# Moving the ends of attention groups ahead of the next scores, re-weighting the filler matmuls, and letting GpSimd make some shifted copies

## The chip, the cores and the metric

The kernel runs on one core of one Trainium2 chip. The metric is the device time in microseconds, the median of three runs. One more execution was taken with the hardware profiler; it has a time of its own.

## The reference

Four layers work on one sequence of 2048 tokens with 512 features and 32 heads of 16 features, in bf16. Each adds its result to x after a layer norm. Layers 0 and 2 (A) are a segmented attention with a memory; layers 1 and 3 (B) are full attention over all tokens.

```python
x = A_x
x = x + _A_ref(_layernorm(x), A_wq, A_wk, A_wv, A_wo, A_beta)
x = x + _B_ref(_layernorm(x), B_wqkv, B_wo)
x = x + _A_ref(_layernorm(x), A_wq, A_wk, A_wv, A_wo, A_beta)
x = x + _B_ref(_layernorm(x), B_wqkv, B_wo)

def _B_ref(x, wqkv, wo):                    # 32 heads, Dh = 16
    q, k, v = ...
    p = _softmax(einsum('bhqd,bhkd->bhqk', q, k) * Dh ** (-0.5))
    return einsum('bhqk,bhkd->bhqd', p, v) ... @ wo

def _A_ref(x, wq, wk, wv, wo, beta):        # 4 segments of 512 tokens
    for s in range(4):
        p = _softmax(einsum('bhqd,bhkd->bhqk', qs, ks) * scale + causal_mask)
        a_dot = einsum('bhqk,bhkd->bhqd', p, vs)
        a_mem = (phi(qs) @ M) / (phi(qs) @ z + 1e-6)
        outs.append(g * a_mem + (1 - g) * a_dot)
        M, z = M + phi(ks).T @ vs, z + phi(ks).sum(tokens)
    return concat(outs) ... @ wo
```

Almost all of the work is the exponential of the scores: 4096 blocks of 128 keys by 512 queries in the two B layers, and fewer masked ones in the A layers.

## The kernel before, in words

**Groups and units.** A `Group` holds, for a layer, a segment of 512 queries, a block `c` of eight heads and a parity `e`, four heads (`r` = 0 to 3) and all their score blocks, called banks (one bank of PSUM, 128 x 512 in f32). The main loop in `attention` makes one unit per turn. A unit takes up to three banks from the groups in order (`take_banks`); `unit` issues their score matmuls on PE (32 rows of contraction, four heads side by side in the array), then one ACT instruction with the exponential of up to 1536 columns into a slot of `pT`. PSUM has two places for scores, banks 0 to 2 and 4 to 6, used in turn, bank 3 (`DXB`) for projections and extra tiles, and bank 7 (`ACC`), where the products with V (PV) of one group add up. `pT` has four slots (`NPU`).

**PV and group ends.** `pv_step` issues the PV matmuls of banks whose exponential was issued two units earlier (three in A layers). When the last bank of a group is done, `pv_close` calls `finish`, which divides by the row sums on DVE and so frees bank 7; a group that still lacks PV work stays in `self.pend`. Only in groups of layer 3 whose keys are taken in one pass (`fm`) is V the stationary operand with 17 columns (32-column tiles of the array); elsewhere the stationary operand is a 128 x 128 block of `pT`, 51 or 34 columns are streamed, and a bank takes four such matmuls. `finish` ends in line 1378 (or 1354 and 1356, where partial sums are kept); `finish_fm` begins with a transpose in line 1396.

**Exponentials on DVE.** To relieve ACT, some banks get their exponential on DVE. `dx_find` and `dx_take` pick one or two, `dx_first` (line 924) turns scores straight into the bits of a bf16 with a multiply and an add, and `dx_chain` (line 970) makes three further copies with a number of `EXP_D` added; PV is then done with all four, so such a bank costs four times the PV matmuls. `dx_room` lets a unit take such banks only while the planner's DVE time stays within `DQ` of the unit's start. `pv_some` issues the PV matmuls of the copies that are ready by the planner's times; without due banks it stops once PE comes within `PVLATE` of ACT.

**The planner.** `Sched.add` records every operation into its engine's list in the order in which Python calls it, with the semaphore waits that follow from buffers and banks; `estimate` keeps a modelled time per engine, by which the code above chooses. So the order on each engine is fixed when the program is built. Each engine works through its list strictly in order.

**Work between the units.** Projections, layer norms, the A layers' memory, and the output projections are generators run by `background`, some before `pv_step` and some after. `keep_busy` closes each turn: if the planner's weighted sum of streamed columns over the last 3413 ns (`Sched.streamed`) is below `FILL`, it issues up to `FILLS` matmuls with a stationary zero block (128 x 512), into bank 7 of the current group or bank 3.

**GpSimd** makes the causal masks of the A layers (line 1283) and, within the B layers, `qm`, the queries with the other parity's heads set to zero (line 1185). `dx_chain` has a branch to put a copy on it, switched off by `POOL_ON = 0`. That branch is open once the A layer 0 is done (`self.wide`).

In the order of one turn the change touches these lines:

```python
self.compose(n, items)              # scores on PE, exponential on ACT, line 924 on DVE
...
if split and (...):
    self.background(True)
self.cr_dve -= self.pv_step(n)      # PV on PE, finish on DVE
self.run_deferred(False)
self.background(...)
...
self.keep_busy()
```

Of the kernel before, what the change touches and what calls it, by code (L numbers as in the profile page):

```python
# [25 lines left out]
LAG = {"pe": 100, "act": 60, "dve": 60, "pool": 70, "sp": 50}  # L26
# [51 lines left out]
class Sched:  # L78
# [1 line left out]

    CW = 0.5

    def __init__(self):
        self.ops = {e: [] for e in ENGS}
        self.t = {e: 0.0 for e in ENGS}
# [3 lines left out]

    def streamed(self, until, ns):

        while self.streams and self.streams[0][0] < until - ns:
            self.streams.pop(0)
        return sum(w for _, w in self.streams) / ns

    def estimate(self, op, ns, gap, tile):
        e = op.eng
        ready = max([d.end + LAG[d.eng] if d.eng != e else d.end + 35 for d in op.deps], default=0.0)  # L100
        if tile is not None:
            rows, r0, cols, c0, n = tile
            st = max(ready, self.pe_issue())
            if cols < 128:
                st = max(st, self.pe_issue() + 30)
            for (a, ar, b, bc, m, at) in self.tiles:
                if ar < r0 + rows and r0 < ar + a and bc < c0 + cols and c0 < bc + b:
                    st = max(st, at + m / 2.4 + (4 if (a, b) == (rows, cols) else 100))
            self.tiles = self.tiles[-11:] + [(rows, r0, cols, c0, n, st)]
            self.t["pe"] = max(self.t["pe"], st + n / 2.4)  # L110
            self.streams.append((st, n / 2.4 * rows / 128 * max(cols / 128, self.CW)))
            op.end = st + n / 2.4 + 170
        elif e == "sp":
            st = max(ready, self.t[e])
            self.t[e] = st + max(gap, 600)
            op.end = st + ns
        else:
            op.end = self.t[e] = max(self.t[e] + gap, ready + ns)
# [140 lines left out]
class Builder:  # L259
# [3 lines left out]
    PART = 2  # L263
    FILL_DVE = 300
    EARLY = 200
    FILL, FILLS = 0.43, 2
    DVE_FIN, DX_FIN = 600, 2500
    EVAC_ACT = 0
    DX_BANK, DX_LATE, BG_BANK, DVE_LATE, DVE_LATE_LOW = 800, 3000, 200, 1500, 9000000000.0
    CR_A, CR_B, CR_W, CR_LOW, CARRY, CARRY_W, REST, NEAR, SLACK = 1300, 1500, 1400, 2200, 0, 0, 14, 10, 300  # L270
    ALT3, ALT5, GAP, AHEAD, PE_B, PE_A, PE_LOW, LOW, PAIRS, TAKEN, PAIRS2 = 2, 4, 3, 500, 4, 3, 4, 24, 60, 3, 1
    NKS = 6
    DX_T, POOL_T, POOL_ON = 430, 1800, 0
    DQN, TAKEN_N, REST_N, NEAR_N, NEAR_W = 600, 3, 14, 100, 24
    DQ, DXS, PVN, PVLATE, PVWAIT, PVHOLE = 3000, 4, 4, 600, 0, 100
    DMA_STEPS, DMA_LATE = 2, 300

    def __init__(self, nc, A_x, A_wq, A_wk, A_wv, A_wo, A_beta, B_x, B_wqkv, B_wo, out):
# [102 lines left out]
        return DmaBatch(self.dsems[self.ring("dsem", 1 << 30)])  # L381


    def keep_busy(self):


        g, n = self.cur, 0
        own = g is not None and g.npv
        if not own and (self.bank_late() > 0 or any(t["next"][0][:1] == ["cont"] for t in self.tasks)):
            return  # L390
        bank, al = (self.banks[ACC], g.acc) if own else (self.banks[DXB], self.new_alloc())
        while n < self.FILLS and self.sc.streamed(max(self.sc.t["pe"], self.sc.t["act"] - 1330), 3413) < self.FILL:
            self.mm(self.ps[:, bank.col0:bank.col0 + 512], self.zero[:, :], self.wB[:, 0, 0:512], not own, not own,
                    [self.b_zero, self.b_wB[0]], bank, al, "fill")
            n += 1
# [556 lines left out]
    def dx_chain(self, k, b0, ents):  # L952


        n = 512 * len(ents)
        w = self.dx_space(b0)[:, 0:n]
        bw = self.b_dxw[b0][:len(ents)]
        hold = [b0] + [self.dx_bufs.pop(0) for _ in EXP_D[1:]]
        for j in range(1, len(EXP_D)):
            if j > 1:  # L960
                yield [], 0, self.DX_T
            b = hold[j]
            o, d = self.dx_space(b)[:, 0:n], float(EXP_D[j])
            wr = [x for i in range(len(ents)) for x in self.dx_writes(b, i)]
            ns = 435 if len(ents) == 2 else 333
            eng = "dve"
            if self.POOL_ON and self.wide and max(self.sc.t["pool"], bw[-1].last_write.end) + self.POOL_T < self.sc.t["dve"] + self.POOL_ON:
                eng, ns = "pool", self.POOL_T if len(ents) == 2 else 700
            self.dx_todo -= 1
            self.op(eng, (lambda o, d: lambda e: e.tensor_scalar(o, w, d, None, op0=ALU.add))(o, d), reads=bw, writes=wr, ns=ns, name="dxs")  # L970
            self.dx_queue(b, ents, j == len(EXP_D) - 1)
        self.dx_now[k] = []
        self.dx_done(b0)
# [533 lines left out]
    def attention(self):  # L1507
# [22 lines left out]
        n = 0  # L1530
        while True:
# [26 lines left out]
            split = not self.low and not isA  # L1558
            self.unit_no = n
            self.units = n  # L1560
            self.compose(n, items)
            self.credit(self.PE_LOW if self.low else self.PE_A if isA else self.PE_B, self.CR_LOW if self.low else self.CR_A if isA else self.CR_W * len(items) / 3 if self.wide else self.CR_B)
            if split and (not self.FIT or not self.wide or self.FIT & 2):
                self.background(True)
            self.cr_dve -= self.pv_step(n)
            self.run_deferred(False)
            self.background(False if split and not (self.FIT & 1 and self.wide) else None)
            if self.step == 2:
# [57 lines left out]
```

## Time and profile before

| | |
|---|---|
| time, median of three runs | 1962.33 us (1961.81 to 1964.88) |
| the profiled execution's own time | 1963.52 us |
| its span, first to last instruction | 1962.0 us |
| mean granted TensorE clock | 0.969 |
| busy: PE, DVE, ACT, POOL | 1752.8, 1523.5, 1822.8, 286.9 us |
| instructions: PE matmuls, DVE, ACT, POOL | 28190, 3240, 1654, 648 |

PE is the matmul engine, PEld its weight loads, ACT the engine of activations, DVE the vector engine, POOL is GpSimd. A line of a group gives source line, engine, operation, output and inputs, shapes, how many; then busy time in us and the mean of one in ns; then the engine's idle time just before them and who ended it. A line of the waits gives who waited for whom, us in total, how often, the longest. A line of the timeline gives start and length in us, and in brackets the idle time of the engine before it. A line of windows gives the stretch, its length, busy us (with instructions) of PE, PEld, DVE, ACT and POOL, then the granted clock, the DMA share and GB/s. Nearly all matmuls go through one helper, line 398, so that they are told apart by operands and shapes.

### The profile page before, as it was taken

How to read it: one execution, taken by the hardware profiler on the slowest of the kernel's cores; microseconds unless marked ns; L12 is line 12 of the kernel's file. 1: busy time of each engine (PE TensorE's matmuls, PEld its weight loads, DVE VectorE, ACT ScalarE, POOL GpSimd, SP SyncE). 2: the span in 40 equal slices, each digit the busy share in tenths (PEclk: the TensorE clock that was granted, in tenths of full speed). 3: DMA queues.
4: the chain of work that ended last, by engine and by line, in shares of the span. 5: the costliest groups of instructions: out<-in, count | busy, mean ns of one | idle time of the engine just before them, and what ended most of it. 6: DMA issues, size and time to landing. Idle time of an engine off the chain costs nothing.

```text
span 1962.0 us, 64238 instructions
## 1 busy us (share of the span) xinstructions
PE 1752.8 (89%) x28190; PEld 902.2 (46%) x28190; DVE 1523.5 (78%) x3240; ACT 1822.8 (93%) x1654; POOL 286.9 (15%) x648
## 2 busy tenths in 40 slices
PE   7889889899989999799998999899998888888887
PEld 3444444556646665466654666555632222222222
DVE  6656566788748797578875788577999999999996
ACT  6789988889999999999989999888999999999998
POOL 3522153110050000500004100231100000000000
PEclk9889998999999999999999899999999989999999
DMA  5110111000100010100011001010000000000000
GB/s 157 25 31 18 29 21 31 14 10 16 16 13 16 5 17 16 23 13 8 11 21 23 5 6 19 13 21 13 9 18 1 1 1 12 1 1 12 1 2 12
DMA packets 94968, 33.49 MB, mean 17 GB/s; under 512 B 87520, under 2 KB 94176, under 8 KB 94688
## 3 DMA queue, kind: packets, MB, share of 16 engines
q1 hardware_dynamic: 94688, 29.39, 7.6%
q8 instruction: 220, 3.60, 0.8%
q14 instruction: 60, 0.49, 0.1%
HBM read 6.30 MB, written 2.10 MB: 4 GB/s over the span
## 4 chain that ended last, share of the span: by engine, by line
PE 44%; ACT 27%; DVE 17%; issue 9%; DMA 1%; POOL 1%; SPq 0%; ACTq 0%; DVEq 0%; POOLq 0%
PE ps L398 44%; ACT pT L1268 26%; DVE dxw L924 3%; DVE dxw L970 2%; POOL pT L1283 1%; DMA xT<-xn 1%; DVE ob L1378 1%; DVE QA L924 1%; DVE VA L924 1%; DVE QA L970 1%; ACT amem L593 1%; DVE VA L970 1%; DVE KA L1396 1%; DVE wA L924 1%; DVE lnst L509 0%
## 5 line engine op out<-in xcount | busy, mean ns | idle before, releaser
L1268 ACT ACTIVATE pT<-ps 128x1536 bf16<-128x1536 f32 (+4 forms) x1612 | 1793.1, 1225 | 110.7 <-PE ps L398 89.3
L398 PE MATMUL ps<-qm,KB 32*128 32x512 bf16 x4096 | 540.4, 392 | 97.6 <-ACT pT L1268 82.1
L398 PEld LDWEIGHTS ps<-VB,pT 128*128 128x128 bf16 x8272 | 280.9, 97 | 217.9 <-issue 130.8
L398 PE MATMUL ps<-VB,pT 128*128 128x51 bf16 (+1 forms) x8272 | 353.7, 187 | 27.8 <-DVE ob L1378 9.9
L924 DVE TENSOR_SCALAR dxw<-ps 128x512 uint16<-128x512 f32 (+1 forms) x335 | 274.1, 821 | 63.2 <-PE ps L398 59.8
L398 PEld LDWEIGHTS ps<-qm,KB 32*128 32x128 bf16 x4096 | 133.8, 91 | 368.0 <-ACT pT L1268 269.5
L1283 POOL TENSOR_SCALAR_AFFINE_SELECT pT<-pT 128x256 bf16<-128x256 bf16 (+2 forms) x517 | 206.7, 419 | 564.2 <-ACT pT L1268 554.7
L1185 POOL TENSOR_SCALAR qm<-QB,par 128x512 bf16<-128x512 bf16 x88 | 73.7, 839 | 1018.2 <-PE ps L398 973.0
L398 PE MATMUL ps<-VB,dxw 128*128 128x51 bf16 (+1 forms) x5144 | 213.6, 186 | 0.4 <-DVE dxw L970 0.3
L398 PE MATMUL ps<-pT,VB 128*17 128x512 bf16 x1133 | 180.8, 391 | 10.7 <-DVE KA L1396 9.8
L398 PEld LDWEIGHTS ps<-VB,dxw 128*128 128x128 bf16 x5144 | 169.5, 96 | 4.5 <-issue 2.2
L970 DVE TENSOR_SCALAR dxw<-dxw 128x1024 uint16<-128x1024 uint16 (+1 forms) x363 | 144.7, 423 | 4.7 <-PE ps L398 3.4
L398 PE MATMUL ps<-qm,KA 32*128 32x128 bf16 (+3 forms) x1024 | 105.9, 313 | 35.6 <-ACT pT L1268 32.0
L398 PE MATMUL ps<-VA,pT 128*128 128x51 bf16 (+1 forms) x2560 | 116.8, 191 | 20.3 <-DVE ob L1378 14.2
L398 PEld LDWEIGHTS ps<-VA,pT 128*128 128x128 bf16 x2560 | 88.4, 98 | 81.6 <-POOL pT L1283 45.4
L398 PEld LDWEIGHTS ps<-pT,VB 128*17 128x17 bf16 x1133 | 41.4, 87 | 122.2 <-issue 103.5
L398 PE MATMUL ps<-dxw,VB 128*17 128x512 bf16 x338 | 93.9, 385 | 0.0
L398 PEld LDWEIGHTS ps<-qm,KA 32*128 32x128 bf16 x1024 | 29.7, 92 | 108.9 <-ACT pT L1268 78.8
L398 PE MATMUL ps<-wB,zero 128*128 128x512 bf16 x225 | 79.6, 411 | 0.0
L924 DVE TENSOR_SCALAR QA<-ps 128x512 uint16<-128x512 f32 (+1 forms) x67 | 59.8, 895 | 21.7 <-PE ps L398 21.1
L398 PE MATMUL ps<-xT,wA 128*128 128x512 bf16 x256 | 71.9, 393 | 2.7 <-DVE xT L555 0.9
L924 DVE TENSOR_SCALAR VA<-ps 128x512 uint16<-128x512 f32 (+1 forms) x75 | 65.2, 872 | 11.6 <-PE ps L398 11.0
(260 smaller groups left out, 2262.5 us busy)
## 6 DMA issues: line engine op xcount, KB each, us to landing
out_dram<-x SPq DMA_DIRECT2D x8, 256.0 KB, 2.2
x<-in_A_x_dram SPq DMA_DIRECT2D x3, 512.0 KB, 8.8
wB<-in_B_wqkv_dram SPq DMA_DIRECT2D x1, 1536.0 KB, 13.1
xT<-xn SPq DMA_TRANSPOSE x60, 2.5
oT<-ob SPq DMA_TRANSPOSE x52, 2.5
x<-in_A_x_dram SPq DMA_DIRECT2D x4, 128.0 KB, 2.2
wA<-in_A_wk_dram SPq DMA_DIRECT2D x1, 512.0 KB, 4.1
wA<-in_A_wq_dram SPq DMA_DIRECT2D x1, 512.0 KB, 5.3
```

The lines of the kernel that those rows point to most:

```text
L398: self.sc.add("pe", lambda e: e.matmul(out, lhsT, rhs, start=start, stop=stop, skip_group_check=True), reads=reads, banks=[(bank, "w", all ...
L593: self.op("act", lambda e: e.activation(et, src, ACT.Exp), reads=bsrc, writes=self.b_amem, ns=1023, gap=915)
L924: self.sc.add("dve", lambda e: e.tensor_scalar(d, o, SCALE * LOG2E * 128, EXP_C, op0=ALU.mult, op1=ALU.add), writes=[w for j in range(k) f ...
L970: self.op(eng, (lambda o, d: lambda e: e.tensor_scalar(o, w, d, None, op0=ALU.add))(o, d), reads=bw, writes=wr, ns=ns, name="dxs")
L1185: self.op(eng, (lambda m, q, col: lambda e: e.tensor_scalar(m, q, col, 0.0, op0=ALU.mult, op1=ALU.add))(m, q, col), reads=[bq, self.b_par] ...
L1268: self.sc.add("act", (lambda dst, src: lambda e: e.activation(dst, src, ACT.Exp, scale=SCALE))(dst, src), writes=self.b_pT[slot * 3 + i:sl ...
L1283: self.op("pool", (lambda blk, pat: lambda e: e.affine_select(blk, blk, pattern=pat, compare_op=ALU.is_ge, fill=0.0, base=0, channel_multi ...
L1378: self.op("dve", lambda e: e.tensor_tensor(ob, src[:, :, 0:16], rb, ALU.mult), reads=[br] + bsrc, writes=[self.b_ob[oi][g.e]], bank=bk, al ...
L1396: self.op("dve", (lambda tk, a: lambda e: e.transpose(tk, a))(tk, src[:, sl]), reads=bsrc, writes=[self.b_tk] + extra, bank=bk, alloc=al, ...
```

## The change

Three edits and their constants. `attention` calls `pv_step` ahead of `compose` when a group is pending or has its last PVs due. `streamed` and `estimate` weigh the matmuls anew, `FILL` goes from 0.43 to 0.5, and `keep_busy` sums the window up to the time at which the next PV work becomes ready. `POOL_ON` goes from 0 to 300: a shifted copy goes to GpSimd if by the planner's times it would end there, at 2900 ns for 1024 columns, no more than 300 ns after DVE's queue. `DQ` goes from 3000 to 2200 and `PVLATE` from 600 to 900. All else is the same code, but since the planner's times move, the built order differs on every engine.

```diff
 class Sched:
-    CW = 0.5
 ...
     def streamed(self, until, ns):
-        while self.streams and self.streams[0][0] < until - ns:
+        while self.streams and self.streams[0][0] < self.pe_issue() - 2 * ns:
             self.streams.pop(0)
-        return sum(w for _, w in self.streams) / ns
+        return sum(w for t, w in self.streams if t >= until - ns) / ns
 ...
-            self.streams.append((st, n / 2.4 * rows / 128 * max(cols / 128, self.CW)))
+            self.streams.append((st, n / 2.4 * (0.285 if rows < 128 else 0.38 if cols < 128 else 1)))
 ...
-    FILL, FILLS = 0.43, 2
+    FILL, FILLS = 0.5, 2
 ...
-    DX_T, POOL_T, POOL_ON = 430, 1800, 0
+    DX_T, POOL_T, POOL_ON = 430, 2900, 300
 ...
-    DQ, DXS, PVN, PVLATE, PVWAIT, PVHOLE = 3000, 4, 4, 600, 0, 100
+    DQ, DXS, PVN, PVLATE, PVWAIT, PVHOLE = 2200, 4, 4, 900, 0, 100
 ...
+    HOR = 0
+
     def keep_busy(self):
 ...
-        while n < self.FILLS and self.sc.streamed(max(self.sc.t["pe"], self.sc.t["act"] - 1330), 3413) < self.FILL:
+        soon = [w.end + LAG[w.eng] for e in self.pvq[:9] if e[0] <= self.unit_no + 1 for w in (self.b_pT[e[4] * 3 + e[5]].last_write,)]
+        at = max(self.sc.t["act"] - 1330, min(soon, default=0.0) - self.HOR)
+        while n < self.FILLS and self.sc.streamed(max(self.sc.t["pe"], at), 3413) < self.FILL:
 ...
             if self.POOL_ON and self.wide and max(self.sc.t["pool"], bw[-1].last_write.end) + self.POOL_T < self.sc.t["dve"] + self.POOL_ON:
-                eng, ns = "pool", self.POOL_T if len(ents) == 2 else 700
+                eng, ns = "pool", self.POOL_T * len(ents) // 2
 ...
+            early = self.pend is not None or self.ends(0)
+            first = self.pv_step(n) if early else 0
             self.compose(n, items)
 ...
-            self.cr_dve -= self.pv_step(n)
+            self.cr_dve -= first if early else self.pv_step(n)
```

## Prediction

> **What bounds the kernel now.** I read the page first, for its busy shares and the clock row.
>
> ```profile
> PE 1752.8 (89%) x28190; PEld 902.2 (46%) x28190; DVE 1523.5 (78%) x3240; ACT 1822.8 (93%) x1654; POOL 286.9 (15%) x648
> ...
> PEclk9889998999999999999999899999999989999999
> ```
>
> ACT carries the time. Then the groups of instructions, with shapes kept apart:
>
> ```profile
> L1268 ACT ACTIVATE pT<-ps 128x1536 bf16<-128x1536 f32 x788 | 1133.9, 1487 | 66.6 <-PE ps L398 53.9 <-POOL pT L1283 5.5 <-issue 0.7
> L1268 ACT ACTIVATE pT<-ps 128x1024 bf16<-128x1024 f32 x654 | 674.2, 1062 | 36.9 <-PE ps L398 28.7 <-POOL pT L1283 2.6 <-ACT pT L1268 0.3
> ```
>
> Neighbouring ACT instructions overlap, so I price them by start to next start where nothing is waited for: 1.330 us for three tiles (1536), 0.903 for two, 0.690 for 768, 0.476 for 512, 0.263 for 256. Over all 1653 instructions that is 1754 us of work; 13 us pass before the first, and the other 195 us are waits, nearly all for PE. By the starts, 50 of them lie before 330 us, 126 between 330 and 1431 us, and 20 in the last stage (layer 3, query segments 1 to 3). Windows over these stages agree, the last with ACT at 518 of 531 us:
>
> ```profile
> 330.00:1431.00 1101.00, 1016.99 (x20032) 639.08 (x20031) 838.65 (x1816) 1024.36 (x934) 154.21 (x338) 0.97 0.08 14
> 1431.00:1962.00 531.00, 456.55 (x4405) 117.90 (x4401) 490.65 (x933) 518.08 (x453) 18.00 (x20) 0.98 0.02 5
> ```
>
> Third, the waits around a group's end (whole span):
>
> ```profile
> PE ps L398 <- DVE ob L1378: 24.0, 30, 2.8
> ...
> PE ps L398 <- DVE KA L1396: 9.8, 20, 0.9
> ...
> PE ps L398 <- DVE KB L1356: 6.3, 10, 1.3
> ```
>
> and one such end in the timeline:
>
> ```profile
> 668.31 0.39 PE L398 MATMUL ps<-qm,KB 32*128 32x512 bf16 x3
> ...
> 668.71 0.25 DVE L1366 RECIPROCAL rd<-ps 128x16 f32<-128x16 f32 x1
> 668.99 0.42 DVE L1378 TENSOR_TENSOR ob<-ps,rd 128x256 bf16<-128x256 f32 x1
> ...
> 669.47 1.00 PE L398 MATMUL ps<-VB,pT 128*128 128x34 bf16 x32 [0.77 <-DVE ob L1378]
> ...
> 669.95 2.07 ACT L1268 ACTIVATE pT<-ps 128x1024 bf16<-128x1024 f32 x2 [1.40 <-PE ps L398]
> ```
>
> The next group's PV matmuls wait for bank 7, which DVE reads until 669.4; ACT then idles 1.40 us.
>
> Last, windows about a clock drop. The first is a full-clock stretch in which PE was busy 2.15 of 3.4 us, the second is what follows:
>
> ```profile
> 435.60:439.00 3.40, 2.15 (x36) 1.08 (x33) 3.33 (x8) 3.33 (x4) 0.00 (x0) 1.00 0.00 0
> 439.00:442.50 3.50, 3.50 (x50) 1.92 (x48) 2.44 (x7) 2.25 (x3) 0.75 (x1) 0.51 0.26 42
> ```
>
> **Part 1, tiles that change engine: +14 us.** Both kernels' instruction lists can be counted. DVE exponentials fall from 895 to 858 tiles (DQ 3000 to 2200, PVLATE 600 to 900), nearly all before the last stage (498 to 460; last stage 397 to 398). ACT takes them: 42 more of 1536, 37 fewer of 1024, 9 more of 256, 7 more of 768, 30 fewer of 512, three fewer evictions. With the periods above: 55.9 - 33.4 + 2.4 + 4.8 - 14.3 - 1.4 = +14.0 us. This lies on the path with no cover. On PE it removes some 435 PV matmuls at 0.026 us (start to start), 11 us. About 57 us of ACT's idle time in the middle follow stretches in which PE was simply at work; 7.6% fewer tiles there give -4 us (0 to -9).
>
> **Part 2, zero matmuls: 225 to 344.** Each holds PE 0.215 us, so 119 cost 25.6 us of PE. They stand after a unit's last PVs and hide in PE's 209 us of idle time; with the cover gone they would push the next scores back. I take +3 us, keep 0 and +26. The gain is the clock. The granted clock is at half for 119 us, in 21 stretches before the end, all starting on one grid of 3.413 us. I added up, for each grid window of the trace, columns / 2.4 ns weighted as the new code weighs them (0.285 for 32-row scores, 0.38 for 32-column PVs, 1 otherwise). The window ahead of a drop held 0.21 to 0.48 of full activity, 17 of the 21 below 0.43; of 517 full-clock windows with no drop behind, 21 were below 0.43. So the gate goes by such a sum. ACT idles 53 us in and right behind the slow stretches; at the rate found elsewhere (0.078 per us) 10 of these would be there anyway, so 43 us hang on the drops. Laid over the ACT work, the new program spends 1.4% of it below 0.35 where the old spends 3.3%, and 3.7% below 0.40 against 6.0%: about half the drops stay. -20 us, bounds 0 and -43.
>
> The Trainium skill (TensorE: Matmul & The Clock Gate, "What's actually happening") says the free-running window is 3413 ns, which agrees, and that the clock falls after an idle window. The windows above were over half busy by the page, so the measured weighting decides. If only idle windows counted, the extra zero matmuls would buy nothing and this term would be 0.
>
> **Part 3, group ends ahead of scores.** If a group's last PVs are due or pending, `pv_step` now runs before `compose`. Counted on PE: between a group's last PV and the next group's first there was one block of scores in 163 of 169 ends; now two blocks in 109 of 167, one in 54. ACT idle within 1.5 us behind a PE wait for a finish adds up to 42 us in the trace; a second block gives DVE's 0.25 + 0.42 us another ACT unit (0.90 or 1.33 us) of cover. 109/167 of 42 is 27, of which I take 24. What is queued behind the moved PVs now is the scores and, for them, ACT. A last burst is now typically 16 PVs, 0.42 us, plus 0.12 to switch: 0.54. ACT is inside another unit then; scores need 0.39 and about 0.1 to wake it. Behind a three-tile unit (1.33) that is covered, behind a two-tile one (0.90) 0.14 us are missing: at some four in ten of 109, +6 us. Also, ACT units that must wait for an old PV to give back a pT slot (four slots) go from 32 to 52; in the middle such a unit idled 11.3/26 = 0.43 us, +9. The sum is -9 us, with -42 (all waits gone) and +59 (109 bursts wholly exposed) as ends.
>
> **Part 4, GpSimd copies: 0.** 254 copies of 1024 and 6 of 512 columns go to POOL, 163 of them in the last stage. No POOL copy exists before. Nearest rows: 0.692 us for an undisturbed `qm` of 512, and 0.307, 0.423, 0.532 us for masks of 128, 256, 384, so about 0.88 ns a column: 1.14 us. The far end is twice the longest `qm` (1.65), 3.3 us. I take 1.14, because it is the same operation on twice the columns. What it costs DVE is in the timeline, POOL then DVE:
>
> ```profile
> 1561.37 0.94 POOL L1185 TENSOR_SCALAR qm<-QB,par 128x512 bf16<-128x512 bf16 x1 [20.86 <-PE ps L398]
> ```
> ```profile
> 1561.41 0.42 DVE L970 TENSOR_SCALAR phq<-dxw 128x1024 uint16<-128x1024 uint16 x1
> 1561.74 0.84 DVE L970 TENSOR_SCALAR dxw<-dxw 128x1024 uint16<-128x1024 uint16 x1
> 1562.50 1.21 DVE L924 TENSOR_SCALAR VB<-ps 128x1024 uint16<-128x1024 f32 x1
> ```
>
> A 0.42 us copy takes 0.84 when POOL is in SBUF; POOL in turn (0.94, not 0.69) waited for the copy before. Reads from PSUM (L924) are never stretched. Over the `qm` rows a DVE copy loses about 0.11 us per POOL instruction, 0.42 at most. With twice the columns the hold is 0.42 + 0.45 = 0.87 us, and the mean loss between 0.2 and 0.11 x (0.87/0.42)^2 = 0.47 us, against the 0.33 us (start to start) that a moved copy saves. In the last stage DVE has 531 - 491 = 40 us free and gains 163 x 0.33 = 54, so it is full only at a loss of 94/163 = 0.58 us each. ACT stays the bound: 0, with -5 (the waits for L924) as the good end.
>
> The Trainium skill (SBUF — State Buffer, "Who interferes with whom") says the shared ports are held for the full instruction. The trace shows less: 0.42 us lost at most against a `qm` of 0.69. By the page the largest loss would be 1.14 us, not 0.87.
>
> **Sum.** +14 - 4 + 3 - 20 - 9 + 0 = -16. The profiled execution took 1963.5 us (span 1962.0 and 1.5 around it), 1.2 above the median of the three runs, so 1947.5 there and 1946 as a median.
>
> **Rivals.**
> *The ports make DVE the bound (slower).* In the last stage a POOL copy starts when its source is written, next to DVE copies or to an L924 of 1.22 us, which hides 1.14 of a hold. From a hold of 1.7 us (a copy of about 2 us undisturbed) the loss passes 0.58. For it: DVE is 92% busy there, and 1.7 lies inside the far end. Against: the 0.88 ns slope. At a loss of 1.0 us: (1.0 - 0.58) x 163 = +68, 2014 us. Chance 0.17.
> *The bursts stall ACT (slower).* If PE is late anyway (92% busy in the middle), the 0.54 us are exposed at most moved ends and little is won back: +30 for -9, 1985 us. Chance 0.11.
> *No clock gain.* The fills miss the bad windows, or the gate counts idle windows or busy share and not the weighted sum: 20 us lost, 1966, or near no change with a little luck in the other terms. Chance 0.10.
> *Both waits go.* Clock -35, ends -25: about 1915. Chance 0.12.
>
> My forecast, 1926 to 1957, has 0.50. The range 1915 to 2000 takes in the cases down to the good one and half of the port case; about 0.15 is left out. Against 0.2% (4 us, about what these runs can tell from no change): faster 0.62, same 0.10, slower 0.28. The likeliest sign's own range is 1915 to 1957.
>
> **What would show it.** Right: ACT work near 1768 us; about ten slow clock stretches; PE's waits for L1378, L1396 and L1356 (L1380, L1398 and L1358 in the new file) under half; POOL copies of 1.1 to 1.8 us; the last stage near 531 us. Wrong: DVE copies at 0.8 us and more by the hundred, POOL copies near 3 us, ACT waits for PE in the last stage well over 5 us, or as many slow clock stretches as now.

## The result, and the profile after

The changed kernel takes 2017.78 us (median of four runs, 2014.31 to 2020.51), and the kernel before 1963.61 us on the same chip: 1.0274 times as long, with a 95% interval of 1.0254 to 1.0295. The forecast was 1946, with a range from 1915 to 2000, and the time lies above it. The profiled execution took 2014.31 us, its span 2012.6; all readings of after are against that one.

The page of after, its busy shares and two rows of the 40 slices:

```profile
PE 1779.2 (88%) x27874; PEld 894.1 (44%) x27874; DVE 1584.0 (79%) x2860; ACT 1830.4 (91%) x1642; POOL 1023.4 (51%) x905
...
POOL 4422325325242214424351174537688788887784
PEclk9999999999999999999999999999999999989999
```

POOL went from 286.9 to 1023.4 us of busy time for 257 more instructions, so that the new copies cannot be 1.14 us long. DVE has 380 instructions fewer, and yet its busy time rose by 60 us. The clock row is better than before in the middle. One of the new copies' groups on POOL, from the groups by form:

```profile
L972 POOL TENSOR_SCALAR dxw<-dxw 128x1024 uint16<-128x1024 uint16 x46 | 131.7, 2863 | 170.6 <-DVE dxw L926 150.9
```

The mean of one is 2863 ns, where the prediction took 1140. The windows over the middle (layers 1 and 2 and the first query segment of layer 3) and the last stage, first the middle of before from the same point, then both of after (the last three columns are clock, DMA share and GB/s):

```profile
316.00:1431.00 1115.00, 1029.93 (x20194) 645.05 (x20194) 844.04 (x1826) 1036.91 (x943) 156.73 (x347) 0.97 0.08 14
```
```profile
318.00:1409.00 1091.00, 1004.25 (x19637) 624.51 (x19635) 821.00 (x1606) 1018.93 (x915) 430.32 (x438) 0.99 0.08 14
1409.00:2012.00 603.00, 501.87 (x4473) 127.14 (x4470) 566.15 (x764) 529.99 (x453) 479.67 (x183) 0.96 0.02 5
```

The middle is 24 us shorter than the 1115 us of before (the 1101 us shown ahead of the result begin 14 us later), and the last stage 72 us longer than the 531: the net loss lies there. DVE issues 169 instructions fewer in it (764 against 933) and is busy 75 us longer (566 against 491). ACT's waits for PE in the last stage, before and then after:

```profile
ACT pT L1268 <- PE ps L398: 5.0, 16, 0.6
```
```profile
ACT pT L1270 <- PE ps L400: 65.2, 115, 2.0
```

And the waits of PE for a group's end, whole span:

```profile
PE ps L400 <- DVE ob L1380: 16.3, 18, 4.1
...
PE ps L400 <- DVE KA L1398: 11.8, 16, 1.6
```

Line 1380 fell by a third (24.0 before); line 1398, nearly all in the last stage, rose (9.8 before), perhaps because DVE reaches it late there, which was not followed up. What a copy on POOL does to DVE is plain in the timeline of after; first POOL, then DVE:

```profile
1702.16 2.93 POOL L972 TENSOR_SCALAR phk<-dxw 128x1024 uint16<-128x1024 uint16 x1
1705.19 2.88 POOL L972 TENSOR_SCALAR QA<-xT 128x1024 uint16<-128x1024 uint16 x1
```
```profile
1702.39 1.25 DVE L972 TENSOR_SCALAR wA<-dxw 128x1024 uint16<-128x1024 uint16 x1
1703.56 0.42 DVE L972 TENSOR_SCALAR xT<-dxw 128x1024 uint16<-128x1024 uint16 x1
1703.90 1.21 DVE L926 TENSOR_SCALAR xT<-ps 128x1024 uint16<-128x1024 f32 x1
...
1706.74 0.42 DVE L972 TENSOR_SCALAR VB<-xT 128x1024 uint16<-128x1024 uint16 x1
1707.07 1.28 DVE L972 TENSOR_SCALAR phq<-xT 128x1024 uint16<-128x1024 uint16 x1
```

DVE's copy at 1702.39 begins 0.23 us after POOL's and takes 1.25 us instead of 0.42. The next begins 1.40 us after POOL's start and loses nothing, as does the one at 1706.74 (1.55 after). The one at 1707.07 (1.88 after) takes 1.28. So a POOL copy has two stretches in which it stops a copy of DVE's, for about 0.85 us each, with a free gap between. The first mostly meets a copy, the second mostly a read from PSUM: of the 160 POOL copies in the last stage, 119 have DVE in a stretched copy 0.6 us after their start, and 115 have it in a line 926 2.3 us after it. Counted over the last stage, 215 of DVE's 439 copies are stretched beyond 0.45 us, by 135 us together, which is 0.84 us for each of the 160 POOL copies there. In the middle 114 of 575 are stretched, by 57 us, 0.58 for each of 99; some 9 of these 57 us are there without the POOL copies too (e1 below). The reads of 1024 columns from PSUM (L926) are at 1.19 to 1.23 throughout.

A table by stages, cut at ACT's own starts, sums it up. ACT idle is what is left of a stage beside ACT's work; slow clock is the time at half the granted clock before the end, with the number of stretches. The last row is the changed kernel without the GpSimd copies (e1 below).

| | first, ACT idle | middle, ACT idle | last, ACT idle | slow clock |
|---|---|---|---|---|
| before | 307, 51 | 1115, 128 | 528, 21 | 119 us, 21 |
| after | 308, 38 | 1091, 106 | 601, 94 | 92 us, 22 |
| after, no GpSimd copies | 312, 42 | 1064, 76 | 527, 18 | 31 us, 7 |

### The profile page after: what moved, and what is told of

Read it like the earlier page. It is cut to its first block, busy times and chain, and to the rows that moved or that the text cites. A ratio compares the mean times of both kernels' runs of the same rounds, so it can differ in the third digit from the quotient of the medians.

```text
span 2012.6 us, 63717 instructions
## 1 busy us (share of the span) xinstructions
PE 1779.2 (88%) x27874; PEld 894.1 (44%) x27874; DVE 1584.0 (79%) x2860; ACT 1830.4 (91%) x1642; POOL 1023.4 (51%) x905
## 4 chain that ended last, share of the span: by engine, by line
DVE 36%; PE 31%; ACT 19%; issue 9%; POOL 4%; DMA 1%; SPq 0%; ACTq 0%; DVEq 0%; POOLq 0%
PE ps L400 31%; ACT pT L1270 18%; DVE dxw L972 5%; DVE dxw L926 4%; POOL pT L1285 2%; DVE QA L972 2%; DVE wA L926 2%; DVE VA L972 2%; DVE wA L972 2%; DVE QA L926 1%; DVE VA L926 1%; DVE VB L972 1%; DVE KB L972 1%; DVE xT L926 1%; DVE VB L926 1%
## 5 line engine op out<-in xcount | busy, mean ns | idle before, releaser
L400 PE MATMUL ps<-VB,pT 128*128 128x34 bf16 (+1 forms) x8416 | 350.7, 187 | 17.1 <-DVE VB L1358 6.4
L926 DVE TENSOR_SCALAR dxw<-ps 128x512 uint16<-128x512 f32 (+1 forms) x278 | 239.8, 869 | 70.3 <-PE ps L400 68.4
L972 POOL TENSOR_SCALAR dxw<-dxw 128x1024 uint16<-128x1024 uint16 x46 | 131.7, 2863 | 170.6 <-DVE dxw L926 150.9
L400 PE MATMUL ps<-VB,dxw 128*128 128x51 bf16 (+1 forms) x4684 | 196.2, 186 | 0.9 <-DVE dxw L972 0.4
L400 PEld LDWEIGHTS ps<-VB,dxw 128*128 128x128 bf16 x4684 | 155.0, 96 | 6.9 <-issue 3.2
L972 DVE TENSOR_SCALAR dxw<-dxw 128x1024 uint16<-128x1024 uint16 (+1 forms) x267 | 127.4, 500 | 1.6
L400 PE MATMUL ps<-VA,pT 128*128 128x51 bf16 (+1 forms) x2560 | 107.2, 188 | 17.4 <-DVE ob L1380 12.8
L400 PE MATMUL ps<-wB,zero 128*128 128x512 bf16 x344 | 116.5, 394 | 3.5 <-DVE x L771 1.5
L972 POOL TENSOR_SCALAR QA<-dxw 128x1024 uint16<-128x1024 uint16 x16 | 45.3, 2833 | 75.6 <-DVE dxw L926 74.4
L926 DVE TENSOR_SCALAR QA<-ps 128x512 uint16<-128x512 f32 (+1 forms) x77 | 68.2, 891 | 16.0 <-PE ps L400 15.7
```

The costliest lines, as they stand in the source:

```text
L400: self.sc.add("pe", lambda e: e.matmul(out, lhsT, rhs, start=start, stop=stop, skip_group_check=True), reads=reads, banks=[(bank, "w", all ...
L926: self.sc.add("dve", lambda e: e.tensor_scalar(d, o, SCALE * LOG2E * 128, EXP_C, op0=ALU.mult, op1=ALU.add), writes=[w for j in range(k) f ...
```

## The experiments

Times are medians; each ratio is to the kernel before on the same chip, whose median was between 1959.8 and 1961.7 in all these comparisons.

### Which part costs, which part gains

Five kernels, each with one part alone or all but one. Three theories: the ports (GpSimd's copies stop DVE's), the bursts at group ends that stall ACT, and the smaller room for DVE's tiles.

e1, the change without the GpSimd copies:

```diff
-    DX_T, POOL_T, POOL_ON = 430, 2900, 300
+    DX_T, POOL_T, POOL_ON = 430, 2900, 0
```

> The changed kernel with POOL_ON = 0 and all else kept: no shifted copy on GpSimd (1284 copies on DVE, 848 DVE tiles, 372 zero matmuls). Theory of the ports (a GpSimd copy of 2.87 us blocks DVE copies for two stretches of about 0.85 us, and DVE, nearly full in the last stage, becomes the bound there): DVE copies are back at 0.42 us, the last stage takes 530 to 537 us again instead of about 600, and the time is about 1945 us (1930 to 1955), faster than the kernel before, because ACT's waits in the first 1430 us fell from 176 to 144 us against 14 us more ACT work. Rival, the bursts ahead of the scores (the order of PV and scores makes ACT wait, whoever copies): the last stage stays above 570 us and the time above 2000. Rival, the smaller room (DQ, PVLATE): also above 1990, since DQ is still 2200.

Measured: 1916.68 us, ratio 0.9765 (0.9735 to 0.9795). That is 28 us better than expected; the port theory's signs in the last stage came out, and the other two theories are ruled out as the cause of the loss. The rest of the change gains 45 us, and the GpSimd copies cost 2017.8 - 1916.7 = 101 us. Its windows show where: the middle is 27 us shorter than in after (1064 against 1091), the last stage 74 (529 against 603), and DVE is busy 76 us less there although it issues 157 instructions more.

```profile
322.00:1386.00 1064.00, 972.90 (x19399) 617.02 (x19556) 783.25 (x1677) 1016.86 (x912) 154.18 (x339) 1.00 0.08 14
1386.00:1915.00 529.00, 458.05 (x4444) 122.39 (x4470) 489.81 (x921) 518.04 (x454) 18.57 (x21) 1.00 0.02 6
```

e2, the kernel before with the GpSimd edit alone:

```diff
-    DX_T, POOL_T, POOL_ON = 430, 1800, 0
+    DX_T, POOL_T, POOL_ON = 430, 2900, 300
-                eng, ns = "pool", self.POOL_T if len(ents) == 2 else 700
+                eng, ns = "pool", self.POOL_T * len(ents) // 2
```

> The kernel before with the GpSimd edit alone (POOL_ON = 300, POOL_T = 2900; 304 copies on GpSimd, 169 of them in the last stage; order of the ends, zero matmuls and room as before). Ports: in the last stage 169 copies at 0.84 us lost and 0.33 saved add 86 us to DVE's 491 busy of 531, so about 45 to 60 us longer there, and about 2015 us in all (2000 to 2040). Bursts: 1955 to 1970, no change, since the ends stand where they stood. Room: no change either.

Measured: 2095.69 us, ratio 1.068 (1.064 to 1.072). The cost, 134 us, is larger than the 101 in the full change and above what was expected. Here 304 copies go to GpSimd instead of 260; the last stage takes 611 us, and the middle 1165 instead of 1115, with ACT idle for 180 us instead of 128. The slow clock rose to 249 us in 49 stretches, and PE stands for 300 us of the span instead of 209.

e3, the ends alone (the lines of `early` and `first` in `attention`, on the kernel before):

```diff
+            early = self.pend is not None or self.ends(0)
+            first = self.pv_step(n) if early else 0
             self.compose(n, items)
...
-            self.cr_dve -= self.pv_step(n)
+            self.cr_dve -= first if early else self.pv_step(n)
```

> The kernel before with the group ends moved ahead of the scores and nothing else (890 DVE tiles, 185 zero matmuls where it had 225). The three edits without GpSimd gave -45 us together where the prediction had -16. If the ends are what was sized too small: PE's waits for the finish lines fall by more than half and the time is 1930 to 1942. If the term was right (-9): 1948 to 1958. If bursts ahead of scores make ACT wait: 1965 or more.

Measured: 1942.27 us, ratio 0.9909 (0.9883 to 0.9935), 17.6 us gained. PE's waits for the finish lines fall as the prediction said: its rows for 1378, 1396 and 1356 from 44.2 us in four rows (24.0 + 9.8 + 6.3 + 4.1) to 18.2 in three, of which the largest is

```profile
PE ps L398 <- DVE ob L1378: 17.4, 19, 4.1
```

The row for line 1396, 9.8 us before, is gone, and the two for 1356, 10.4 before, are at 0.8. The rival of the bursts, by which the time would have risen, falls.

e4, the weighted sum and the fills alone (`streamed`, `estimate`, `FILL` 0.5, `soon` and `at`, on the kernel before):

```diff
-    FILL, FILLS = 0.43, 2
+    FILL, FILLS = 0.5, 2
...
+            self.streams.append((st, n / 2.4 * (0.285 if rows < 128 else 0.38 if cols < 128 else 1)))
```

> The kernel before with the new weights, FILL 0.5 and the look-ahead of keep_busy and nothing else (391 zero matmuls, 895 DVE tiles). If the clock is what was sized too small (its term was -20 + 3): slow clock falls from 119 us to 40 or less and the time is 1925 to 1937. If the term was right: about half the drops left, 1940 to 1950. If zero matmuls do not hold the clock: 20 drops or so as before, 1960 or more.

Measured: 1961.82 us, ratio 1.0008 (0.9989 to 1.0026), no difference. The clock did what was intended: the slow time fell from 119 to 75 us, and the page's clock row has two slices below 9 instead of five:

```profile
PEclk9889999999999999999999999999999999999999
```

The time did not follow: the middle takes 1115 us as before, and ACT idles 126 us in it, against 128. ACT's idle time in the slow stretches and up to 1 us behind them fell from 49 to 33 us over the whole span, and elsewhere it rose from 155 to 166. The added zero matmuls may have part in that: idle time with one in it, or up to 0.6 us ahead of it, went from 36 to 44 us.

e5, `DQ` 2200 and `PVLATE` 900 alone:

```diff
-    DQ, DXS, PVN, PVLATE, PVWAIT, PVHOLE = 3000, 4, 4, 600, 0, 100
+    DQ, DXS, PVN, PVLATE, PVWAIT, PVHOLE = 2200, 4, 4, 900, 0, 100
```

> The kernel before with DQ 2200 and PVLATE 900 and nothing else (855 DVE tiles for 895, ACT work 1767 us for 1754). By the prediction's terms (+14 on ACT, -4 on PE) about 1972 (1968 to 1976). If the lighter PE and DVE lists win back more than ACT takes on, so that this hides part of the -45: 1940 to 1958.

Measured: 1964.57 us, ratio 1.0031 (1.0006 to 1.0056), 4.8 us lost, between what the two theories had expected. The slow clock rose to 150 us.

### Where the GpSimd copies cost

The same condition, closed for one of the two stages. `fm` is true for layer 3's groups of one pass, which fill the last stage.

```diff
-            if self.POOL_ON and self.wide and max(
+            if self.POOL_ON and self.wide and not ents[0][0].fm and max(       # e7
+            if self.POOL_ON and self.wide and ents[0][0].fm and max(           # e8
```

> The changed kernel with GpSimd copies only for groups whose V is streamed (not fm), that is only ahead of the last stage: 98 copies on GpSimd, 1 in the last stage. Ports, with DVE's fill deciding: DVE is 76% busy there, so that the blocked time is hidden; within 10 us of the kernel without GpSimd copies, some 1940 to 1960. Rival, every blocked copy costs time wherever it stands (an equal share of the loss for each of the 260): 98/260 of about 72 us, 27 us above the kernel without copies.

> The changed kernel with GpSimd copies only for fm groups, that is in the last stage alone: 163 copies there. Ports, with DVE's fill deciding: nearly the whole loss, 60 to 75 us above the kernel without GpSimd copies, 2005 to 2020. Equal share of the loss for each copy: 163/260 of about 72 us, 45 us above it, about 1990. Bursts: as long as the changed kernel whatever is on GpSimd.

Measured: e7 1949.10 us, ratio 0.994 (0.9915 to 0.9964), 32 us above e1 for 98 copies, 0.33 each. e8 1978.79, ratio 1.0083 (1.0056 to 1.011), 62 above e1 for 163 copies, 0.38 each. So the cost is nearly even over the copies, and against the expectation it isn't hidden in the middle, where DVE is only 75% busy. An explanation is order: PE takes its matmuls in the order of its list, and where the next one needs a DVE result that is late, it waits, though DVE has time to spare elsewhere. PE's and PEld's waits for DVE's exponentials (L926, into the `dxw` tiles) over the whole span, e1 ahead of e7:

```profile
PEld ps L400 <- DVE dxw L926: 12.1, 27, 0.8
...
PE ps L400 <- DVE dxw L926: 5.1, 17, 0.7
```
```profile
PEld ps L400 <- DVE dxw L926: 20.7, 40, 1.7
PE ps L400 <- DVE dxw L926: 10.4, 23, 1.5
```

Within the middle, PE and PEld wait 28.3 us for these tiles instead of 12.4, and for line 926 into any tile 45.6 instead of 21.6; waits of the two can overlap, so these are not us of the result. On ACT, the idle time of the middle, counted in gaps over 0.02 us, is 105 us instead of 73. Of that, 20 us instead of 8 lie within 1.5 us behind a wait of PE for DVE's exponentials, and 16 instead of 7 behind a wait for a group's finish; the other 12 us of the rise follow no such wait and stay open. In the last stage it is DVE's time itself, as the window of e8 shows, with DVE 95% busy:

```profile
1382.00:1971.00 589.00, 483.72 (x4409) 126.02 (x4438) 561.89 (x766) 526.58 (x452) 482.56 (x183) 0.98 0.02 5
```

Here the expectation, 60 to 75 us above the kernel without copies, came true (62). The two costs add up to 94 of the 101 us.

### Ports, lateness or the planner

Three explanations for 0.33 to 0.38 us a copy remained: the copies stop DVE's (ports); a copy that comes after 2.9 us instead of 0.4 makes its PV matmuls late (lateness); the planner, which doesn't know that DVE is held up, decides wrongly (order).

e9 is e1 with 167 GpSimd instructions in the last stage that nobody reads: an addition in place on `amem`, 1024 columns of uint16, at about the places where after has its copies. DVE keeps all its copies.

```diff
+            if self.wide and ents[0][0].fm and len(ents) == 2 and j == 1 and self.ring("dum", 6) < 5:
+                am = self.amem[:, :, :, :].rearrange("p a b c -> p (a b c)").bitcast(dt.uint16)
+                self.sc.add("pool", lambda e: e.tensor_scalar(am, am, 22.0, None, op0=ALU.add), writes=self.b_amem,
+                            deps=[x.last_write for x in bw], name="dum", ns=2870)
```

> The changed kernel with POOL_ON = 0 and 167 more GpSimd instructions of the copies' form (uint16, 1024 columns, in place on a buffer that the last stage does not use, one behind 5 of 6 pairs of tiles there) whose result nobody reads; DVE makes every copy itself, as in the kernel without GpSimd copies. Ports: the last stage loses about 0.84 us per such instruction and is relieved of nothing, about +100 to +140 us on 1917, at 2020 to 2055. Rival, PE waits for copies that come late from GpSimd: nobody waits for these, so 1912 to 1925. Rival, the planner's order with GpSimd in it is the worse one: the order is that of the kernel without copies, so 1912 to 1925 too.

Measured: 2052.94 us, ratio 1.0475 (1.0458 to 1.0491), 136 us above e1 or 0.82 for each instruction. Nothing waits for these instructions, and in the trace DVE and ACT work through the same instructions in the same order as in e1 (PE too, but for neighbours that start nearly together), so neither lateness nor order explains any of it. Nor does lateness show elsewhere: in after, e7 and e8 no wait of PE or PEld for a copy on POOL is on the list. The window of the last stage has it all; DVE is 96% busy there with nearly the instructions of e1 (923 for 921):

```profile
1385.00:2049.00 664.00, 534.24 (x4440) 135.17 (x4468) 636.71 (x923) 537.43 (x454) 494.15 (x188) 0.93 0.01 4
```

DVE's busy time in that stage rose by 147 us over e1, and its idle time fell from 39 us (529 - 490) to 27 (664 - 637). So the stage is 135 us longer, and DVE could not be filled entirely. The timeline, POOL's line ahead of DVE's:

```profile
1702.95 2.95 POOL L973 TENSOR_SCALAR amem<-amem 128x1024 uint16<-128x1024 uint16 x1 [0.15 <-DVE woA L926]
```
```profile
1703.19 1.26 DVE L976 TENSOR_SCALAR VB<-QA 128x1024 uint16<-128x1024 uint16 x1
1704.37 0.41 DVE L976 TENSOR_SCALAR phk<-woA 128x1024 uint16<-128x1024 uint16 x1
```

It is the same pattern as in after: 0.24 us into GpSimd's instruction 1.26, then 1.42 us into it 0.41.

e10 is a program of its own that measures the disputed rows alone, without any other work. `u` is the shifted copy, `b` the bf16 form of `qm`, `f` a DVE read from PSUM:

```python
u: e.tensor_scalar(dst[:, i, 0:w], src[:, 0:w], 22.0, None, op0=ALU.add)                       # uint16
b: e.tensor_scalar(pd[:, i, 0:w].bitcast(bf), src[:, 0:w].bitcast(bf), col[:, 0:1], 0.0, op0=ALU.mult, op1=ALU.add)
f: e.tensor_scalar(vd[:, i, :], ps[:, 0:1024], 22.0, 1.0, op0=ALU.mult, op1=ALU.add)
```

> Computes none of the attention; it measures copies by themselves: on GpSimd alone six uint16 adds of 1024 columns, six of 512, then six and six of the qm form in bf16; then twelve DVE copies alone; then GpSimd uint16 copies of 1024 beside 36 DVE copies; beside 14 DVE reads of PSUM; then bf16 of the qm form beside 36 DVE copies. Ports: a uint16 copy alone takes about 2.77 us for 1024 and 1.49 for 512 columns, bf16 about 1.1 and 0.69, so the length belongs to the type and not to waiting; DVE copies beside it lose up to 0.85 us twice per GpSimd copy, reads of PSUM lose nothing. If the length came from waiting for DVE: about 1.1 us alone for uint16 too.

Measured, GpSimd alone: uint16 takes 2.769 us for 1024 columns and 1.489 for 512; the bf16 form takes 1.123 and 0.697. GpSimd's timeline, in which six of 1024 and six of 512 columns stand in each line:

```profile
2.00 26.43 POOL L254 TENSOR_SCALAR pd<-src 128x1024 uint16<-128x1024 uint16 x12 [1.58 <-DVE col L246]
28.52 10.63 POOL L259 TENSOR_SCALAR pd<-src,col 128x1024 bf16<-128x1024 bf16 x12
```

So the prediction's 1.14 us was right to 2% for 1024 columns of the `qm` form, and wrong by a factor of 2.4 for the copies, and waiting for DVE is no part of that. The two forms differ in the element type and in the operation (an add of a constant, a multiply and add with a column); which of the two sets the length is not shown. Beside DVE copies without a pause it is GpSimd that loses, against the expectation; DVE was first there, and its line ahead of POOL's is:

```profile
39.19 5.12 DVE L254 TENSOR_SCALAR vd<-src 128x1024 uint16<-128x1024 uint16 x15 [36.14 <-POOL pd L259]
43.39 14.61 POOL L254 TENSOR_SCALAR pd<-src 128x1024 uint16<-128x1024 uint16 x1 [4.24 <-DVE vd L254]
```

GpSimd's copy took 14.61 us instead of 2.77. DVE's run of 48 copies ended at 55.38 without a loss (0.337 us from start to start), and GpSimd's copy 2.62 us later, nearly its whole undisturbed length. Beside DVE reads from PSUM it took 2.77 and neither lost. Beside bf16 GpSimd instructions (1.53 us instead of 1.12) every second DVE copy took 1.26. So the loss of a single DVE copy, 0.84 us, is the same beside both forms. A uint16 copy on GpSimd can cause it twice; in after's last stage the mean is one loss a copy, since a PSUM read mostly lies over the second hold.

e15 asks how much the planner's ignorance costs. For each copy that goes to GpSimd it adds what DVE loses to DVE's modelled time:

```diff
                 eng, ns = "pool", self.POOL_T * len(ents) // 2
+                self.sc.t["dve"] += 420 * len(ents)
```

> The changed kernel, but the planner adds 420 ns per tile (840 for two) to its DVE time when it gives a copy to GpSimd; 169 copies go there, 76 of them in the last stage, and 825 tiles to DVE. It tells the loss of DVE time itself from the planner's not knowing of it. Loss of DVE time: about 0.38 us each as before, 169 x 0.38 = 64 us above the kernel without copies, less the few us that fewer tiles shift, some 1970 to 1990. Planner not knowing: PE is ordered for a DVE that really is late, so most of the loss goes, 1925 to 1945.

Measured: 1968.63 us, ratio 1.0037 (1.0016 to 1.0057), 52 us above e1. It is 49 us better than after, though mostly because fewer copies go to GpSimd (169 in all, 76 in the last stage). About 13 of the 52 us are more ACT work, as only 825 tiles still go to DVE; what is left is 0.23 us a copy. That is less than 0.33 to 0.38, so order may have a share, but the smaller one (not a clean measure, since fewer copies also stand farther apart): also with a planner that knows, each copy moved costs more than it saves.

### Where the 45 us come from

e3, e4 and e5 alone add up to a gain of 11 us (17.6 - 2.0 - 4.8), and e1 gained 45. The pairs show which two work together.

```diff
 e6:  e3 and e4, GpSimd off              e11: e3 and e5            e12: e4 and e5
 e13: e3 and DQ 2200 (PVLATE 600)        e14: e3 and PVLATE 900 (DQ 3000)
 e16: e1 with DQ 3000 (PVLATE 900)       e17: the kernel before with PVLATE 900
```

> Moved ends and new zero matmuls, the room as in the kernel before, no GpSimd copies (882 DVE tiles, 372 zero matmuls). One at a time the three edits gave -17, 0 and +5 us; together -45. Clock theory: the new weights hold the clock only where the ends no longer leave PE standing, so this pair has most of it: slow clock under 60 us, 1920 to 1932. Lists theory (fewer tiles let PE and DVE keep up, and the moved ends use that): this pair adds only its parts, 1940 to 1950. Simple sum of the parts: 1943.

> Moved ends and the smaller room, zero matmuls as in the kernel before, no GpSimd copies (846 DVE tiles, 204 zero matmuls). Lists theory: most of the -45 is here, 1920 to 1932. Clock theory: slow clock stays above 90 us and the time is 1942 to 1955. Simple sum: 1947.

> New zero matmuls and the smaller room, the ends where they were (858 DVE tiles, 396 zero matmuls). If the moved ends are needed for all of it: 1957 to 1970, with PE's waits for the finish lines as long as before. If clock and room alone carry the -45: 1925 to 1940. Simple sum: 1965.

> Moved ends with DQ at 2200 and PVLATE still 600 (874 DVE tiles; zero matmuls and GpSimd as in the kernel before). Ends alone gave 1942 us, ends with both constants 1923. If the room for new tiles on DVE is what works with the moved ends: 1922 to 1930. If PVLATE is: 1938 to 1946.

> Moved ends with PVLATE at 900 and DQ still 3000 (860 DVE tiles). If PVLATE is what works with the moved ends (fewer PV matmuls of DVE tiles when PE is close behind ACT, so that the scores are in time): 1922 to 1930. If DQ is: 1938 to 1946. If it takes both: both kernels between 1930 and 1940.

> The changed kernel without GpSimd copies and with DQ back at 3000, PVLATE left at 900 (860 DVE tiles, 350 zero matmuls). If PVLATE and the ends carry the gain and DQ nothing beside them: 1912 to 1922, as without GpSimd copies (1917). If DQ adds its 10 us there too: 1925 to 1932.

> The kernel before with PVLATE at 900 and nothing else (864 DVE tiles). If PVLATE works only with the moved ends (where PV matmuls of DVE tiles now stand ahead of scores): 1955 to 1968. If it works by itself: 1935 to 1948.

| kernel | us | ratio, interval | DVE tiles | middle, ACT idle in it | slow clock |
|---|---|---|---|---|---|
| e3 ends | 1942.27 | 0.9909 (0.9883 to 0.9935) | 890 | 1089, 118 | 116 us |
| e17 PVLATE | 1952.49 | 0.9961 (0.9944 to 0.9978) | 864 | 1112, 114 | 160 us |
| e13 ends, DQ | 1932.51 | 0.9848 (0.9821 to 0.9876) | 874 | 1072, 93 | 82 us |
| e14 ends, PVLATE | 1924.24 | 0.9811 (0.9785 to 0.9837) | 860 | 1073, 89 | 79 us |
| e11 ends, both | 1923.45 | 0.9790 (0.9755 to 0.9826) | 846 | 1071, 82 | 96 us |
| e6 ends, fills | 1945.03 | 0.9906 (0.9870 to 0.9942) | 882 | 1090, 115 | 55 us |
| e12 fills, both | 1968.46 | 1.0030 (1.0009 to 1.0051) | 858 | 1107, 105 | 92 us |
| e16 e1, DQ 3000 | 1918.88 | 0.9801 (0.9778 to 0.9824) | 860 | 1068, 84 | 44 us |
| e1 all but GpSimd | 1916.68 | 0.9765 (0.9735 to 0.9795) | 848 | 1064, 76 | 31 us |

The ladder of the gain is then: ends 18 us; `PVLATE` 900 on top of them 18 more (e14); `DQ` nothing beside it (e11, e16), though 10 where `PVLATE` stays at 600 (e13, between what its two theories had expected); the fills 7 more (e11 to e1) or 5 (e14 to e16), in both pairs with intervals that overlap. `PVLATE` alone gains 8 (e17, between what the two theories had expected of it), so with the ends it brings about 10 more than its own share. With the ends where they were, `DQ` 2200 on top of it loses 12 (e17 to e5). ACT's idle time in the middle falls from 118 us (e3) to 89 (e14). An explanation is that `pv_some` then puts fewer PV matmuls of DVE's tiles ahead of scores that ACT will soon need, which matters more once the due ones go first. This is argued, not shown: no run changed the order of this work and left the number of tiles alone.

The fills do the same on three bases (before to e4, e3 to e6, e5 to e12): less slow clock (119 to 75, 116 to 55, 150 to 92 us), no less time. And e17 is 8 us faster than before with 41 us more slow clock. Only where the middle had already been eased (e11 to e1, e14 to e16) may some of it pay.

## Why the prediction was wrong, point by point

**GpSimd copies, 0 taken, 101 us measured.** This is the step that failed, in two terms. The first is the length: 1.14 us came from the `qm` and mask rows, "because it is the same operation on twice the columns". It is not: type and operation differ, and e10 measured 1.12 for the one and 2.77 for the other. The far end of 3.3 us contained the truth; the planner's own constant in the diff (2900 ns) was close to it, and was given no weight. From the length came the hold, 0.87 us where two of 0.85 stand, and from that the mean loss, 0.2 to 0.47 where the trace of after has 0.84 in the last stage and 0.58 in the middle. The second term is the free time: "40 us free" in the last stage took DVE as one that can be filled to 100%. In the four runs in which DVE binds that stage it is busy 93 to 96% of it (e2 570 of 611, after 566 of 603, e8 562 of 589, e9 637 of 664). At that share of 531 us there are 3 to 19 us free beside its 491, not 40, and the break-even lies at (3 to 19 + 54)/163 = 0.35 to 0.45 us a copy instead of 0.58. With the measured numbers the formula is consistent, though the fill of 94 to 96% comes from these same runs: DVE's work in e1's last stage, 490, less 160 x 0.33 for the moved copies, plus the 135 of the stretches, is 572 us, and at 94 to 96% this needs 596 to 609 us; 603 were measured.

A third thing was missing altogether: a cost in the middle (27 us), where DVE has time to spare and the prediction took none. e7 shows the cost, and PE's longer waits for DVE with it; that the order of PE's list is the reason is argued.

The Trainium skill (SBUF — State Buffer, "Who interferes with whom") says that whoever issues first gets the shared pair for the whole instruction while the other fully blocks. The prediction set the measured 0.42 us against that. As to blocking the trace agrees: a DVE copy that meets a hold stands still for 0.84 us. As to the whole instruction it doesn't: DVE's copies that begin 1.1 to 1.7 us after the start of a POOL copy are not stretched (0 of 141), and the longest copy of DVE's in after took 1.73 us, far from a loss of all of the 2.87.

**The rival of the ports** had chance 0.17 and the figure 2014. Mechanism and signs were right: copies near 3 us, DVE copies stretched by the hundred, ACT waiting for PE in the last stage. Its figure came near 2017.8 by luck, by two errors that cancel: it priced 68 us where 101 were lost (74 in the last stage and 27 in the middle, for which it had nothing), and it stood on a forecast 29 us too slow for the rest (1946 against 1917).

**Zero matmuls, -17 taken (+3 and -20), nothing measured on the kernel before (e4).** The premise that the clock falls after windows of little activity held, though the weighted sum isn't singled out: in before, 19 of the 21 windows ahead of a drop have PE busy for less than 70%, and 23 of the 516 other full-clock windows. With the new weights the slow time falls in e4 from 119 to 75 us, so that 63% of it stay where half was taken, and 31 us stay in e1. In after itself 22 stretches stay instead of the ten forecast, where the kernel without the GpSimd copies has 7: there PE waits 78 us for DVE's exponentials and copies instead of 11. The step that failed here is "43 us hang on the drops". In e4 ACT idles 16 us less in and right behind slow stretches and 11 us more elsewhere. The likeliest reading is that this idle time was mostly not caused by them: where PE waits, ACT idles, and a window later the clock drops, so that with fewer drops the waits stay. Part of the 11 us can be the added zero matmuls (8 us at most, by the idle time with one near it); no run separates the two. The Trainium skill's rule that the clock falls after an idle window (TensorE: Matmul & The Clock Gate, "What's actually happening"), taken as the only way, would have made this term 0 for another reason. The term did come out near 0, but the rule does not fit the traces: in after, too, the windows ahead of 21 of 22 drops were partly busy, PE for 18 to 74% of them, with weighted sums of 0.05 to 0.47 (in the one other PE did nothing), and more zero matmuls did take slow time away.

**Group ends, -9 taken, -18 measured (e3), -36 with `PVLATE`.** The direction was right and the size half of what came; which term was off stays open. Counted as the prediction counted it, ACT's idle time within 1.5 us behind a PE wait for a finish fell by 33 us in e3 (51 to 18), where 24 were taken, and 15 came back elsewhere, since all of ACT's idle time fell by 18 (204 to 186, in gaps over 0.02 us): that is as much as the +6 for bursts and the +9 for slots of `pT` together. Within 0.7 us it fell by 17 (31 to 15), and then nothing came back.

**Tiles, +14 - 4 taken.** The count was right: ACT's work rose from 1754 to 1768 us by the starts in the trace. What failed is that `PVLATE` was read only by the number of tiles it moves to ACT and the PV matmuls that go with them: on top of the ends it gains 18 us net (e14). That this comes from work taken from in front of the scores is the explanation argued above. e5 without the ends loses 4.8 (1 to 11), which +10 fits.

**The sum** was -16; measured were +54, which e1 divides into -45 and +101 (the 2 us between are the difference of the kernel before on two chips). Without the GpSimd copies the time is at the good end of the range (1917 for 1915), but not by the way of that rival, which gave 35 us of gain to the clock.

## What to carry to other kernels

Price an operation that is moved to another engine by a row of that engine with the same element type and operation, and if there is none, let the sum run at the far end too: here the same columns took 2.77 us in one form and 1.12 in another. An engine that another one's instructions can stop may lose more time than the work that is taken off it, so compare the stretch that a moved instruction causes (0.84 us) with what it saves (0.33), and don't count on filling a stage entirely (DVE reached 93 to 96% here). Idle time that coincides with a slow clock is not yet due to it; a run that cuts the slow clock and changes nothing else is what tells (e4, as far as added zero matmuls allow).

The version to keep is e1, the change with `POOL_ON = 0`: 1916.68 us, 2.35% below the kernel before (2.05 to 2.65%).

## What the runs showed of the hardware that had not been expected

- GpSimd's `tensor_scalar` with uint16 in and out (an add) takes 2.769 us for 128 x 1024 and 1.489 for 128 x 512, with bf16 (multiply and add) 1.123 and 0.697.
- A uint16 GpSimd copy of 2.87 us stops DVE's copies between SBUF buffers twice, for about 0.85 us each: in after, DVE copies that begin 0.1 to 0.3 us after its start take 1.25 us on average (132 of 132 stretched), those at 1.1 to 1.7 us take 0.42 (0 of 141), those at 1.9 to 2.1 take 1.17 on average (26 of 27). DVE's reads of 1024 columns from PSUM took at most 1.23 us, with and without such copies.
- DVE copies back to back held GpSimd off until they ended: one copy of 2.77 us took 14.61 (e10, seen once).
- The slow clock could be cut by more than a third (119 to 75 us) without any effect on the time (ratio 1.0008).
